# A fused attention and soft-MoE kernel: ScalarE takes a part of the reads of a shared PSUM tile, and a transpose gets 64 columns

## The chip, the cores and the metric

The kernel runs on one core of one Trainium2 chip. A core has a matrix engine (TensorE, PE in the profile, whose weight loads are listed as PEld), a vector engine (VectorE, DVE), a scalar engine (ScalarE, ACT), GpSimd (POOL), and SyncE (SP), which here only issues transfers. Each engine works through its own queue in order and waits for others on semaphores. TensorE writes its products into PSUM, from where VectorE or ScalarE carry them into SBUF.

The metric is the time of one execution on the device in microseconds (us), lower being better; the time before is the median of three runs.

## What is computed

Attention over 8 batches of 12 heads, 448 tokens and 64 columns a head, and then a soft mixture of experts over all 8 x 448 = 3,584 tokens of 768 columns. Cut to what matters:

```python
scores = q @ k.T / 8, masked above the diagonal
x = softmax(scores) @ v                      # (3584, 768), the heads side by side
logits = x @ phi                             # phi is 768 x 32
d = exp(logits - logits.max(0)); d /= d.sum(0) + 1e-09
slot_input = d.T @ x                         # 32 slots, 4 for each of 8 experts
slot_out[e] = relu(slot_input[e] @ w1[e]) @ w2[e]
c = exp(logits - logits.max(1)); c /= c.sum(1) + 1e-09
out = c @ slot_out                           # (3584, 768)
```

The first softmax of the logits runs over all tokens, so the kernel keeps a running maximum, a running sum and a running `d.T @ x` from batch to batch, and rescales them.

## The kernel before

The 96 heads are worked in 48 pairs; `block(p)` handles pair p, and six pairs make a batch. Every call on an engine goes through a helper in line 67 that keeps program order, so all rows of the profile name line 67, and one goes by the names of tiles.

A block does the following for its two heads. The scores stand in three PSUM tiles `s0`, `s1`, `s2` of 1,024 f32 columns, taken in turn. A first round of products (`scores1`, rows `s<-tri,identb` for the mask and `s<-qd,ks` for the scores) starts two heads ahead; VectorE takes column maxima out of it (`max_keys`, rows `r<-s`), TensorE turns them (`max_row`, rows `rt<-ident,r` and `s<-ident,r`), VectorE makes the row maximum (`mr`), GpSimd spreads it (`max_spread`), and a second round of products (`scores2`, rows `s<-r,k`) subtracts it within PSUM. ScalarE takes the exponential (`exps`, rows `pt<-s`), TensorE multiplies with v (`attv_pair`, rows `po<-va,pt`), VectorE divides by the sums (`norm`) and writes `x`. A block begins with the `s<-r,k` products of its first head: its head, below.

Of each finished pair, x is turned so that logits can be taken: `xtrans` makes four transposes of 128 x 128 into the PSUM tile `xm`, each with a part of x as the weights and the identity as what is moved, and `xcopy` carries 512 columns into `xt` in SBUF by ScalarE. A pair has 448 tokens: the last of the four parts of x has 64 rows and zeros below.

**The shared tile.** After the second head's exponential its score tile is free for a short while. Under the name `m = s_[(a + 1) % 3]` it takes the small products at the end of the block, and the next block then overwrites it with `scores1`, beginning with the mask `s<-tri`. What m holds goes by p % 6, from the second batch on; `mr` reads it in every block, first of all:

| p % 6 | products in m | read by VectorE after `mr` |
|---|---|---|
| 0 | sum over tokens for the previous batch's second half (`dispatch_a`, `s<-x,gs`), 384 columns from 0 | `dispatch_b`: `si`, 384 columns |
| 1, 5 | logits of two pairs (`logits_a`), columns 0 to 127 | `logits_t`: adds them to `lt` |
| 2 | turned `gs` and `lt` (`logits_e`) | copies into `gs` and `lg` |
| 3 | logits of the first two pairs; sum over tokens, first 128 columns of the first half, from column 512 | `lt` = logits + `mk` (which holds the mask of the last 64 tokens), then `si`, 128 columns |
| 4 | sum over tokens, the other 256 columns, from 512 | `si`, 256 columns |

The turned maxima for `mr` stand in the last 128 columns. `dispatch_b` computes `si = si * al + m`. The rows for p % 6 = 0 and 4 with sums occur six times each (p = 12 to 42 and 10 to 40), those of 3 seven times (p = 9 to 45). The last pair has a function of its own, `last_block`.

What orders the work is program order on each engine, and semaphores that the build puts between engines wherever two of them use one tile.

The first 24 pieces of the expert weights are loaded during the blocks. The others go into memory that the attention part frees: their transfers wait for its last products and then run one after the other to the end of the expert part. After `early.close()` a filler tile `pad` of `PAD` columns stands ahead of them.

Of the kernel before, what the change touches and what calls it, by code (L numbers as in the profile page):

```python
# [9 lines left out]
F32 = mybir.dt.float32  # L10
F32R = mybir.dt.float32r
BF16 = mybir.dt.bfloat16
AF = mybir.ActivationFunctionType
ALU = mybir.AluOpType
# [3 lines left out]
P = 128  # L18
NB, NH, S, HD = 8, 12, 448, 64
# [7 lines left out]
NCH = 4  # L27
# [6 lines left out]
NR, XB, XT = 2, 3, 2  # L34
RES, TW1, LATE2 = 24, 11, 4

HT = 2
WN, PAD = 1536, 192
WARM = (2, 3, 3)
START = (9, 6, 2, 4)  # L40

# [41 lines left out]
def attention_soft_moe(ctx: ExitStack, tc: tile.TileContext, qk, va, phi, w, out):  # L83
    nc = _Core(tc)
    const = ctx.enter_context(tc.tile_pool(name="const", bufs=1, side="left"))
# [4 lines left out]
    xtp = early.enter_context(tc.tile_pool(name="xtp", bufs=1, side="right"))  # L90
# [22 lines left out]
    x_[1] = moe.tile([P, NCH, 3 * P], F32, name="x1")  # L113
    x_[2] = moe.tile([P, NCH, 3 * P], F32, name="x2")
    x_[0] = moe.tile([P, NCH, 3 * P], F32, name="x0")
    ltn = moe.tile([P, P + 1], F32, name="lt")
    lt = ltn[:, 0:P]
    gs = moe.tile([P, P], F32, name="gs")
    mk = moe.tile([P, P], F32, name="mk")

    st = {"w": 0}
# [69 lines left out]
    ident = const.tile([P, P], F32, name="ident")  # L191
# [15 lines left out]

    for x in (x_[1], x_[0], x_[2]):
        nc.vector.memset(x[:, NCH - 1], 0.0)
    nc.scalar.activation(out=identb, in_=ident, func=AF.Copy)  # L210
    load_qk(2, 0)
    nc.gpsimd.memset(r2[0:64, :, :].bitcast(F32), 0.0)
# [210 lines left out]
    def xtrans(p):  # L423
        x, xm = st.pop(("x", p)), misc(f"xm{p}")
        st["xm", p] = xm
        for c in range(NCH):
            nc.tensor.transpose(out=xm[:, P * c:P * c + P], in_=x[:, c], identity=ident)

    def xcopy(p):
        xt = st["xt", p] = xtp.tile([P, 512], F32, tag="xt", name=f"xts{p}", bufs=XT)  # L430
        if p == NPAIR - 3:
            nc.vector.tensor_copy(out=xt, in_=st.pop(("xm", p)))
        else:
            nc.scalar.activation(out=xt, in_=st.pop(("xm", p)), func=AF.Copy)

    def logits_a(b, js, g, first=True, last=True):

# [5 lines left out]

    def logits_t(j, g):

        nc.vector.tensor_tensor(out=lt, in0=g, in1=lt if j else mk, op=ALU.add)

    def logits_b(b):

# [36 lines left out]
    def dispatch_b(b, hf, sp, sl=slice(0, 384)):  # L486
        s = si[:, 384 * hf + sl.start:384 * hf + sl.stop]
        nc.vector.scalar_tensor_tensor(out=s, in0=s, scalar=st["al", b][:, 0:1], in1=sp[:, 0:sl.stop - sl.start],
                                       op0=ALU.mult, op1=ALU.add)
# [8 lines left out]
    phis = [const.tile([P, 3, NSLOT], F32, tag="ph", name=f"phi{hf}", bufs=2) for hf in range(2)]  # L498
    run_m = [const.tile([P, 1], F32, name=f"run_m{i}") for i in range(2)]
    run_z = const.tile([P, 1], F32, name="run_z")  # L500
    lg = const.tile([P, NB, NCH, NSLOT], F32, name="lg")


# [16 lines left out]
    copy_k2(0, h0)  # L520
    sub_k(0, h0, nc.vector)
    nc.vector.memset(pob, 0.0)
    for t, v in ((mk, 0.0), (mk[96:P, 64:P], -1.0e30), (ltn[:, P:P + 1], -1.0e30), (run_m[1], 1.0e30), (run_z, 0.0)):
        nc.vector.memset(t, v)
    sub_q(0, h0)
    scores1_all(0)
# [37 lines left out]
    def block(p):  # L564
        a, b = 2 * p, p // 6 - 1
        m6 = p % 6
        if p + 1 < NPAIR:
            loads_v(p + 1, nc.sync if p + 1 < NPAIR - 1 else nc.scalar)
        if p % 2 and p < 44 or p in (16, 30):
            load_w(st["w"])  # L570
            st["w"] += 1

        if p:
            norm(p - 1, 2)
        scores2(a, range(NCH))
        exps(a)
        if p == 0:
            copy_k2(0, h1)
            cast_q(1, h1)
            warm(START[3], pob)  # L580
            max_row(1, 0)
            max_row(1, 1)
            max_spread(1)
            sub_k(1, h1, nc.vector)
        elif p > 1:
            xcopy(p - 2)
            if p == NPAIR - 2:
                sub_q(p + 1, h0)
        scores1_all(a + 2)
        if p == 0:  # L590
            warm(START[2], pob)
        for k in range(3):
            max_keys(a + 2, k)
        if p == 0:
            cast_k(2, h0)
        scores2(a + 1, range(NCH))
        exps(a + 1)
        if p == 0:
            cast_k(2, h1)
        scores1_all(a + 3)  # L600
        if m6 == 2 and p > 6:
            logits_b(b)
        max_keys(a + 3, 0)
        late_k = p == 1
        if p == 1:
            sub_q(2, h0)
            sub_k(3, h0)
            sub_q(2, h1)
            load_qk(4, 0)
        elif p:  # L610
            sub_k(p + 2, h0 if late_k else slice(0, 2))
            if not late_k:
                load_qk(p + 4, 1)
            sub_q(p + 1, h1 if p == NPAIR - 2 else slice(0, 2))
            load_qk(p + 3, 0)
        else:
            sub_q(1, h0)
            sub_q(1, h1)
            load_qk(3, 0)
            sub_k(2, h0)  # L620
        copy_k2(p + 1)
        if m6 == 2 and p > 6:
            logits_d(b, lt)
        if p:
            cast_k(p + 3)
            cast_q(p + 2)
        else:
            cast_q(2)
            cast_k(3)
        if m6 == 3 and p > 6:  # L630
            logits_al(b)
        elif m6 == 4 and p > 6:
            logits_n(b)
        attv_pair(p)
        max_row(a + 2, 1)
        max_spread(a + 2)
        if p == 0:
            sub_k(2, h1)
            load_qk(4, 1)
        for k in (1, 2):  # L640
            max_keys(a + 3, k)
        for k in range(2):
            norm(p, k)

        m = s_[(a + 1) % 3]
        parts = []
        if m6 in (1, 3, 5) and p > 1:
            j = (m6 + 3) % 6
            logits_a(b if m6 == 1 else p // 6, (j, j + 1), m[:, 0:P])
        elif m6 == 2 and p > 6:  # L650
            logits_e(b, m, 0)
        if m6 == 3 and p > 6:
            parts = [(b, 0, slice(0, P), 512)]
        elif m6 == 4 and p > 6 and p < NPAIR - 2:
            parts = [(b, 0, slice(P, 3 * P), 512)]
        elif m6 == 0 and p > 6:
            parts = [(b - 1, 1, slice(0, 3 * P), 0)]
        for d, hf, sl, o in parts:
            dispatch_a(d, hf, m[:, o:o + sl.stop - sl.start], sl)
        max_row(a + 3, 0, to=m[:, 1024 - P:1024])  # L660
        max_row(a + 3, 1)
        if m6 == 2 and p > 6:
            logits_e(b, m, 1)
        max_spread(a + 3)
        if late_k:
            sub_k(p + 2, h1)
            load_qk(p + 4, 1)
        if m6 in (1, 3, 5) and p > 1:
            logits_t(j, m[:, 0:P])
        for d, hf, sl, o in parts:  # L670
            dispatch_b(d, hf, m[:, o:o + sl.stop - sl.start], sl)
        if p:
            xtrans(p - 1)

# [7 lines left out]
    i, b, p = NHD - 1, NB - 1, NPAIR - 1  # L682
# [5 lines left out]
    x, sm = x_of(p), moe.tile([P, 2 * NCH], F32, tag="sm", name=f"sm{i}", bufs=2)  # L688
# [17 lines left out]
    for c in range(NCH):  # L706
        n = P if c < NCH - 1 else AW
        nc.scalar.activation(out=x[0:n, c, 0:HD], in_=pa[0:n, c, 0:HD], func=AF.Copy, scale=sa[0:n, c:c + 1])
    xtrans(p - 1)
    xcopy(p - 1)  # L710
    xa = xtp.tile([P, 512], F32, tag="xt", name="xta", bufs=XT)

    def last_xt(k):
        for c in (2 * k, 2 * k + 1):
# [294 lines left out]
```

## Time and profile before

| | us |
|---|---|
| median of three runs | 395.83 (395.76 to 396.35) |
| the profiled execution | 396.08 |
| its span in the profile | 394.4 |
| mean granted TensorE clock | 0.979 of full speed |

The blocks end near 300 us in the span; the expert part follows. A block takes about 6 us. In a row of the timeline the first number is the start in us from the beginning of the span, the second the length in us, then come the engine, the line, the operation, output<-input by the names of tiles, the shapes, and, in brackets, how long the engine stood idle ahead of it and which instruction seems to have ended that. In a row of the groups the count stands after x, then the busy time in us, the mean length of one in ns, and the idle time ahead. A plain f32 product is listed as two records, a transpose as one.

### The profile page before, as it was taken

Reading aid. Unit: us, or ns where it says so; the run is one execution under the profiler, and the core shown is the slowest. Engines: PE = TensorE matmul, PEld = TensorE weight load, DVE = VectorE, ACT = ScalarE, POOL = GpSimd, SP = SyncE. Lnnn points to the kernel's source line nnn. Section 1 sums busy time; section 2 is a strip of 40 time slices with the busy share of each in tenths; the row PEclk is TensorE's granted clock in tenths of the full one; section 3 lists DMA queues with packets and bytes.
Section 4 is the critical chain, followed back from the end, with each engine's and each line's share of the span. In section 5 each row is a group of like instructions: output and inputs, shape, how many; then the busy total and the mean of one; then the engine's idle time right before and its main releaser. Section 6 shows DMA issues by size and latency. Waiting matters only on the chain.

```text
span 394.4 us, 13997 instructions
## 1 busy us (share of the span) xinstructions
PE 366.3 (93%) x5763; PEld 293.9 (75%) x5763; DVE 295.2 (75%) x835; ACT 282.9 (72%) x397; POOL 256.5 (65%) x215
## 2 busy tenths in 40 slices
PE   7899999999999999999999999999999989988940
PEld 3689889888988998898889888988986544533420
DVE  7887889888888888898888988888886675342550
ACT  5888899898898898888988988888864012431440
POOL 5998899898898888898988988889860000000000
PEclk9999999999999999999999999999999999998985
DMA  7868877788898788777997877887579999999996
GB/s 250 277 229 281 288 288 237 251 273 274 274 318 272 244 270 300 257 246 248 307 323 256 286 240 249 275 287 250 183 246 399 422 431 428 429 421 419 433 429 295
DMA packets 28720, 119.17 MB, mean 302 GB/s; under 512 B 3440, under 2 KB 3952, under 8 KB 26480
## 3 DMA queue, kind: packets, MB, share of 16 engines
q1 hardware_dynamic: 28512, 118.01, 83.2%
q8 instruction: 45, 0.74, 0.7%
q10 hardware_dynamic: 144, 0.27, 0.2%
q14 instruction: 19, 0.16, 0.1%
HBM read 107.25 MB, written 11.01 MB: 300 GB/s over the span
## 4 chain that ended last, share of the span: by engine, by line
PE 67%; DMA 9%; POOL 9%; DVE 5%; ACT 4%; issue 2%; SPq 0%; POOLq 0%; DVEq 0%; ACTq 0%
PE s L67 34%; PE po L67 20%; DMA w<-in_w_dram 8%; POOL r L67 6%; PE xm L67 4%; POOL ks L67 3%; PE so L67 2%; PE e L67 2%; PE pp L67 2%; PE rt L67 2%; DMA kraw<-in_qk_dram 1%; ACT qd L67 1%; DVE lm L67 1%; DVE lg L67 1%; ACT w L67 1%
## 5 line engine op out<-in xcount | busy, mean ns | idle before, releaser
L67 DVE TRANSPOSE_TENSOR_REDUCE r<-s 128x32 f32<-128x1024 f32 x96 | 119.5, 1245 | 7.7 <-PE s L67 4.9
L67 ACT ACTIVATE pt<-s 128x1024 f32<-128x1024 f32 x96 | 98.8, 1029 | 31.0 <-PE s L67 24.0
L67 PEld LDWEIGHTS po<-va,pt 128*64 128x64 f32 x3008 | 102.3, 138 | 11.8 <-issue 11.3
L67 PE MATMUL po<-va,pt 128*64 128x65 f32 x3008 | 109.2, 224 | 0.0
L67 POOL TENSOR_TENSOR r<-qraw,qd 64x896 fp32r<-64x896 f32 (+1 forms) x50 | 99.4, 1989 | 1.9 <-ACT qd L67 1.8
L67 POOL TENSOR_TENSOR ks<-kraw,ks 64x896 fp32r<-64x896 f32 (+1 forms) x48 | 89.7, 1870 | 4.1 <-ACT ks L67 0.5
L67 POOL TENSOR_SCALAR_AFFINE_SELECT r<-mr 14x448 fp32r<-14x448 f32 x96 | 61.6, 643 | 32.9 <-DVE mr L67 28.6
L67 PE MATMUL s<-qd,ks 128*66 128x64 f32 (+3 forms) x384 | 80.6, 321 | 0.0
L67 PE MATMUL s<-r,k 128*128 128x448 f32 (+3 forms) x384 | 65.2, 291 | 2.7 <-POOL r L67 2.7
L67 PEld LDWEIGHTS s<-r,k 128*128 128x128 f32 (+1 forms) x384 | 59.3, 176 | 8.6 <-POOL r L67 5.9
L67 PEld LDWEIGHTS s<-qd,ks 128*128 128x128 f32 (+1 forms) x384 | 52.5, 183 | 2.1 <-issue 0.9
L67 ACT ACTIVATE ks<-kraw 128x896 fp32r<-128x896 f32 (+1 forms) x49 | 45.0, 920 | 5.6 <-DMA kraw<-in_qk_dram 4.4
L67 ACT ACTIVATE k<-ks 64x896 fp32r<-64x896 f32 (+1 forms) x49 | 45.8, 936 | 1.2
L67 ACT ACTIVATE qd<-qraw 128x896 fp32r<-128x896 f32 (+1 forms) x48 | 44.6, 929 | 0.9 <-POOL r L67 0.7
L67 PE MATMUL s<-tri,identb 128*128 128x192 bf16 x192 | 39.6, 270 | 0.6
L67 DVE TENSOR_REDUCE r<-r 128x16 f32<-128x32 f32 x192 | 33.7, 176 | 5.0
L67 DVE TENSOR_REDUCE mr<-s 14x32 f32<-14x128 f32 x47 | 13.1, 279 | 21.4 <-ACT qd L67 14.8
L67 PE MATMUL xm<-ident,x 128*128 128x128 f32 x188 | 28.3, 273 | 0.0
L67 ACT ACTIVATE xts<-xm 128x512 f32<-128x512 f32 x46 | 27.2, 591 | 0.4 <-PE xm L67 0.4
L67 DVE TENSOR_SCALAR x<-po,sm 64x64 f32<-64x64 f32 x94 | 25.9, 276 | 0.7
L67 DVE COPY w<-pp 128x384 f32<-128x384 f32 x28 | 14.5, 553 | 15.4 <-PE pp L67 15.3
L67 DVE TENSOR_TENSOR x<-po,sm 128x384 f32<-128x384 f32 x47 | 25.2, 537 | 0.0
(151 smaller groups left out, 397.9 us busy)
## 6 DMA issues: line engine op xcount, KB each, us to landing
w<-in_w_dram SPq DMA_DIRECT2D x34, 768.0 KB, 6.7
kraw<-in_qk_dram SPq DMA_DIRECT2D x46, 448.0 KB, 4.4
qraw<-in_qk_dram SPq DMA_DIRECT2D x46, 448.0 KB, 4.5
w<-in_w_dram SPq DMA_DIRECT2D x5, 3072.0 KB, 25.0
va<-in_va_dram SPq DMA_DIRECT2D x47, 260.0 KB, 4.8
out_dram<-w SPq DMA_DIRECT2D x7, 1536.0 KB, 12.6
w<-in_w_dram SPq DMA_DIRECT2D x5, 1536.0 KB, 11.2
qk<-in_qk_dram SPq DMA_DIRECT2D x2, 448.0 KB, 7.1
```

Source lines behind the costliest of these rows:

```text
L67: return self._tc.keep_in_program_order(op(*args, **kwargs))
```

## The change

The reads of m are split between two engines, some additions are put off, and the fourth transpose of x is made narrower.

- **Logits.** For the first two pairs of a batch (p % 6 = 3) ScalarE copies the logits from m into `lt`, in place of VectorE's addition of `mk`. The mask is put in a block later, as a memset of `lt[96:P, 64:P]` by VectorE (p % 6 = 4). The two memsets that filled `mk` at the start go.
- **Sums over tokens.** VectorE adds the first 128 columns into `si` out of m. The others (128 columns at p % 6 = 4, 256 at p % 6 = 0) ScalarE copies into a new tile `scr` in SBUF, and VectorE adds them in the next block, after `norm`'s first two steps and ahead of `mr`.
- **Transpose.** The fourth part of x is turned by a plain f32 product with 64 columns of the identity in place of a transpose with 128; `xcopy` carries 448 columns. The `xt` tiles are two fixed ones, whose last 64 columns are zeroed at the start.
- `PAD` goes from 192 to 128 columns. The transfers of the late weights wait for the same instructions in both.

```diff
-WN, PAD = 1536, 192
+WN, PAD = 1536, 128
...
+    xt_ = [xtp.tile([P, 512], F32, name=f"xt{k}") for k in range(XT)]
...
+    for x in xt_:
+        nc.vector.memset(x[:, S:], 0.0)
...
         for c in range(NCH):
-            nc.tensor.transpose(out=xm[:, P * c:P * c + P], in_=x[:, c], identity=ident)
+            if c < NCH - 1:
+                nc.tensor.transpose(out=xm[:, P * c:P * c + P], in_=x[:, c], identity=ident)
+            else:
+                nc.tensor.matmul(xm[:, P * c:S], x[:, c], ident[:, 0:S - P * c], start=True, stop=True)
...
-        xt = st["xt", p] = xtp.tile([P, 512], F32, tag="xt", name=f"xts{p}", bufs=XT)
+        xt = st["xt", p] = xt_[p % XT]
...
-            nc.scalar.activation(out=xt, in_=st.pop(("xm", p)), func=AF.Copy)
+            nc.scalar.activation(out=xt[:, 0:S], in_=st.pop(("xm", p))[:, 0:S], func=AF.Copy)
...
-        nc.vector.tensor_tensor(out=lt, in0=g, in1=lt if j else mk, op=ALU.add)
+        if j:
+            nc.vector.tensor_tensor(out=lt, in0=g, in1=lt, op=ALU.add)
+        else:
+            nc.scalar.activation(out=lt, in_=g, func=AF.Copy)
...
+    scr = const.tile([P, 2 * P], F32, name="scr")
...
-    for t, v in ((mk, 0.0), (mk[96:P, 64:P], -1.0e30), (ltn[:, P:P + 1], -1.0e30), (run_m[1], 1.0e30), (run_z, 0.0)):
+    for t, v in ((ltn[:, P:P + 1], -1.0e30), (run_m[1], 1.0e30), (run_z, 0.0)):
...
+        for d, hf, sl in st.pop("rest", ()):
+            dispatch_b(d, hf, scr, sl)
+        if m6 == 4:
+            nc.vector.memset(lt[96:P, 64:P], -1.0e30)
...
         for d, hf, sl, o in parts:
-            dispatch_b(d, hf, m[:, o:o + sl.stop - sl.start], sl)
+            n = sl.stop - sl.start - P
+            dispatch_b(d, hf, m[:, o:o + P], slice(sl.start, sl.start + P))
+            if n:
+                nc.scalar.activation(out=scr[:, 0:n], in_=m[:, o + P:o + P + n], func=AF.Copy)
+                st["rest"] = ((d, hf, slice(sl.start + P, sl.stop)),)
```

How the instructions stand after the build is shown at two places. A bracket names the semaphores that an instruction waits for, each by the engine or the transfer queue that raises it (`DVE_49` is raised by VectorE, `Activation_49` by ScalarE).

The first place is the seam from pair 30 (p % 6 = 0) to pair 31; m is `s_80` there. On ScalarE before, from the end of pair 30's casts into pair 31:

```order
L67 ACTIVATE k_92<-ks_87 64x2x448
L67 ACTIVATE ks_87<-kraw_83 128x2x448 [waits DMAHW4_49,PE_49,Activation_49]
L67 ACTIVATE qd<-qraw_84 128x896 [waits DMAHW5_49,Pool_49]
L67 ACTIVATE pt_94<-s_81 128x1024 [waits DVE_49,PE_49]
L67 ACTIVATE xts_3271<-xm_3256 128x512
```

and with the change:

```order
L67 ACTIVATE qd<-qraw_84 128x896 [waits DMAHW5_49,Pool_49]
L67 ACTIVATE scr<-s_80 128x256 [waits DVE_49,PE_49]
L67 ACTIVATE pt_94<-s_81 128x1024 [waits PE_49]
L67 ACTIVATE xt_101<-xm_3250 128x448
L67 ACTIVATE pt_95<-s_79 128x1024 [waits PE_49]
```

The copy into `scr` stands between the cast of `qd` and the new block's exponential, and waits for VectorE; the value that it waits for is that of VectorE's 128-column sum out of the same tile. On TensorE before, at the same seam, from the head to the overwriting of m:

```order
L67 MATMUL s_81<-r_93,k_92 128x448 [waits Activation_49,Pool_49]
L67 MATMUL s_81<-r_93,k_92 128x320
L67 MATMUL s_81<-r_93,k_92 128x192
L67 MATMUL s_81<-r_93,k_92 66x64
L67 LDWEIGHTS identb
L67 MATMUL s_80<-tri_117,identb 128x192 [waits DVE_49]
```

and with the change, from the last use of m in pair 30 on:

```order
L67 MATMUL s_80<-ident,r_91 76x128 [waits DVE_49]
L67 MATMUL xm_3250<-ident,x_99 128x128 [waits PE_49]
L67 MATMUL xm_3250<-ident,x_99 128x128 x2
L67 MATMUL xm_3250<-ident,x_99 128x64
L67 MATMUL s_81<-r_93,k_92 128x448 [waits Activation_49,Pool_49]
L67 MATMUL s_81<-r_93,k_92 128x320
L67 MATMUL s_81<-r_93,k_92 128x192
L67 MATMUL s_81<-r_93,k_92 66x64
L67 LDWEIGHTS identb
L67 MATMUL s_80<-tri_119,identb 128x192 [waits Activation_49]
```

The mask product that overwrites m now waits for ScalarE's copy, where it waited for VectorE's sum; and the fourth product of `xm` has 64 columns.

The second place is the end of pair 33 (p % 6 = 3); m is again `s_80`. On VectorE before:

```order
L67 RECIPROCAL sm_3539<-sm_3539 128x7 [waits DVE_49]
L67 TENSOR_REDUCE mr_3555<-s_80 14x32 [waits PE_49,Activation_49,Pool_49]
L67 TENSOR_TENSOR lt<-s_80,mk 128x128
L67 SCALAR_TENSOR_TENSOR si<-si,al_3498,s_80 128x128 [waits Activation_49]
L67 TENSOR_TENSOR x_98<-po,sm_3539 128x2x3x64 [waits DVE_49]
```

and with the change, VectorE first:

```order
L67 RECIPROCAL sm_3531<-sm_3531 128x7 [waits DVE_49]
L67 TENSOR_REDUCE mr_3547<-s_80 14x32 [waits PE_49,Activation_49,Pool_49]
L67 SCALAR_TENSOR_TENSOR si<-si,al_3490,s_80 128x128 [waits Activation_49]
L67 TENSOR_TENSOR x_98<-po,sm_3531 128x2x3x64 [waits DVE_49]
L67 TENSOR_SCALAR x_98<-po,sm_3531 64x64 x2
```

then ScalarE at the same place:

```order
L67 ACTIVATE qd<-qraw_88 128x896 [waits DMAHW0_49,Pool_49]
L67 ACTIVATE al_3490<-run_m_150,run_m_149 128x1
L67 ACTIVATE lt<-s_80 128x128 [waits DVE_49]
L67 ACTIVATE pt_94<-s_81 128x1024 [waits PE_49]
L67 ACTIVATE xt_100<-xm_3552 128x448
```

The addition into `lt` has left VectorE's queue, and ScalarE's copy waits for VectorE's `mr`. VectorE's sum waited for ScalarE before too, for `al`; with the change the value that it waits for is that of the copy into `lt`.

More of the change, by code (lines that the diff above doesn't have):

```diff
@@ L426, in xtrans @@
         for c in range(NCH):
-            nc.tensor.transpose(out=xm[:, P * c:P * c + P], in_=x[:, c], identity=ident)
+            if c < NCH - 1:
+                nc.tensor.transpose(out=xm[:, P * c:P * c + P], in_=x[:, c], identity=ident)
+            else:
+                nc.tensor.matmul(xm[:, P * c:S], x[:, c], ident[:, 0:S - P * c], start=True, stop=True)
     def xcopy(p):
-        xt = st["xt", p] = xtp.tile([P, 512], F32, tag="xt", name=f"xts{p}", bufs=XT)
+        xt = st["xt", p] = xt_[p % XT]
         if p == NPAIR - 3:
-            nc.vector.tensor_copy(out=xt, in_=st.pop(("xm", p)))
+            nc.vector.tensor_copy(out=xt[:, 0:S], in_=st.pop(("xm", p))[:, 0:S])
         else:
-            nc.scalar.activation(out=xt, in_=st.pop(("xm", p)), func=AF.Copy)
+            nc.scalar.activation(out=xt[:, 0:S], in_=st.pop(("xm", p))[:, 0:S], func=AF.Copy)
     def logits_a(b, js, g, first=True, last=True):
@@ L710, in attention_soft_moe @@
     xcopy(p - 1)
-    xa = xtp.tile([P, 512], F32, tag="xt", name="xta", bufs=XT)
+    xa = xt_[p % XT]
     def last_xt(k):
```

## The prediction

> **What bounds the kernel now.** First the head of the page.
>
> ```profile
> span 394.4 us, 13997 instructions
> PE 366.3 (93%) x5763; PEld 293.9 (75%) x5763; DVE 295.2 (75%) x835; ACT 282.9 (72%) x397; POOL 256.5 (65%) x215
> PE 67%; DMA 9%; POOL 9%; DVE 5%; ACT 4%; issue 2%; SPq 0%; POOLq 0%; DVEq 0%; ACTq 0%
> ```
>
> The span and the shares of the chain that ended last say: TensorE is the bound, with other engines in the chain for short pieces. The profiled execution took 396.08 us, 1.7 more than its span; the median is 395.83. After the last block the chain is one long stretch of weights.
>
> ```profile
> 326.46 30.39 DMA w<-in_w_dram
> ```
>
> Those loads start as attention lets go of its buffers, so whatever the blocks lose or win moves the end by as much. The question is what one block loses. The next view is the timeline around the seam from pair 30 (p%6 = 0) to pair 31, columns start, length, engine.
>
> ```profile
> 197.49 0.30 PE L67 MATMUL s<-ident,r 128*76 128x128 f32 x1
> 197.52 0.47 PEld L67 LDWEIGHTS xm<-ident,x 128*128 128x128 f32 x4
> 197.93 0.28 DVE L67 TENSOR_REDUCE mr<-s 14x32 f32<-14x128 f32 x1 [0.72 <-ACT qd L67]
> 197.99 0.71 PE L67 MATMUL s<-r,k 128*128 128x448 f32 x4
> 198.14 0.59 DVE L67 SCALAR_TENSOR_TENSOR si<-si,al,s 128x384 f32<-128x384 f32 x1
> 198.78 0.24 PE L67 MATMUL s<-tri,identb 128*128 128x192 bf16 x1
> ```
>
> The first row is the old block's last use of the shared tile m; 0.50 later the new block's head (`s<-r,k`) starts, and then the mask product `s<-tri` must overwrite m. It starts at 198.78, 0.05 after VectorE's sum ends at 198.73: VectorE's reading of m holds TensorE. An unheld seam, pair 31 to 32:
>
> ```profile
> 203.62 0.31 PE L67 MATMUL s<-ident,r 128*76 128x128 f32 x1
> 204.12 0.72 PE L67 MATMUL s<-r,k 128*128 128x448 f32 x4
> 204.28 0.27 DVE L67 TENSOR_TENSOR lt<-s,lt 128x128 f32<-128x128 f32 x1
> 204.68 0.26 PE L67 MATMUL s<-tri,identb 128*128 128x192 bf16 x1
> ```
>
> Here m is free at 204.55, and the mask comes at 204.68, 0.56 after the head and 1.06 after `s<-ident,r`: TensorE's own pace. Counted from `s<-ident,r`, the mask of pair 31 comes at 1.29, so it loses 0.23. The other two seams with sums, 33 to 34 and 34 to 35:
>
> ```profile
> 215.56 0.30 PE L67 MATMUL s<-ident,r 128*76 128x128 f32 x1
> 216.00 0.28 DVE L67 TENSOR_REDUCE mr<-s 14x32 f32<-14x128 f32 x1 [0.73 <-ACT qd L67]
> 216.21 0.27 DVE L67 TENSOR_TENSOR lt<-s,mk 128x128 f32<-128x128 f32 x1
> 216.41 0.33 DVE L67 SCALAR_TENSOR_TENSOR si<-si,al,s 128x128 f32<-128x128 f32 x1
> 216.79 0.24 PE L67 MATMUL s<-tri,identb 128*128 128x192 bf16 x1
> ```
>
> ```profile
> 221.62 0.30 PE L67 MATMUL s<-ident,r 128*76 128x128 f32 x1
> 222.06 0.37 ACT L67 ACTIVATE run_z<-run_z,bs,al 128x1 f32<-128x1 f32 x1
> 222.07 0.28 DVE L67 TENSOR_REDUCE mr<-s 14x32 f32<-14x128 f32 x1 [0.51 <-ACT qd L67]
> 222.28 0.46 DVE L67 SCALAR_TENSOR_TENSOR si<-si,al,s 128x256 f32<-128x256 f32 x1
> 222.79 0.24 PE L67 MATMUL s<-tri,identb 128*128 128x192 bf16 x1
> ```
>
> Masks 1.23 and 1.17 after `s<-ident,r`: losses of 0.17 and 0.11. These three waits, six or seven times each, are all that the split of the reads can win: 6 x 0.23 + 7 x 0.17 + 6 x 0.11 = 3.2 us.
>
> **The reads, part by part.** The rows of the built order decide. ScalarE's copy `scr<-s` waits for VectorE and PE, `lt<-s` waits for VectorE, and the mask of pair 31 now waits for ScalarE. The two engines do not read m side by side: each waits for the other's read. The shortened VectorE sum is followed by a ScalarE copy in line. Prices:
>
> ```profile
> L67 ACT ACTIVATE xta<-e 128x256 f32<-128x256 f32 x1 | 0.4, 377 | 0.0
> L67 ACT ACTIVATE mk<-e 128x128 f32<-128x128 f32 x1 | 0.3, 277 | 0.2 <-PE e L67 0.2
> 310.95 0.29 DVE L67 TENSOR_TENSOR lg<-lg,lm 128x128 f32<-128x128 f32 x1
> 311.28 0.31 ACT L67 ACTIVATE lg<-lg 128x128 f32<-128x128 f32 x1 [1.71 <-DVE lg L67]
> 311.62 0.29 DVE L67 TENSOR_REDUCE lm<-lg 128x4 f32<-128x128 f32 x1 [0.37 <-ACT lg L67]
> ```
>
> A sum of 128 columns takes 0.33 (the row at 216.41), ScalarE's PSUM copies 0.38 (256 columns) and 0.28 (128). The other rows price a hand-over: 311.28 − 311.24 = 0.04 to ScalarE, 311.62 − 311.59 = 0.03 back; to TensorE 0.05, as above.
>
> - 30 to 31: sum 198.14 to 198.47; ScalarE 198.51 to 198.89; mask 198.94 instead of 198.78: **+0.16**, 6 times.
> - 33 to 34: `mr` ends 216.28; `lt` copy 216.32 to 216.60; VectorE's sum, which waits for ScalarE, 216.63 to 216.96; mask 217.01 instead of 216.79: **+0.22**, 7 times.
> - 34 to 35: sum 222.28 to 222.61; ScalarE (its queue is free at 222.43) 222.65 to 222.93; mask 222.98 instead of 222.79: **+0.19**, 6 times.
>
> Together 0.96 + 1.54 + 1.14 = 3.6 us. Queued behind each copy on ScalarE is the new block's exponential, which needs the head's products (0.71 from the head, the row at 197.99); the copies end 0.90, 0.54 and 0.81 after a head that stands 0.50 behind `s<-ident,r`. So it starts at most 0.2 late, still no later than the mask, and I take the mask's delay alone. Were a hand-over free, each seam would lose 0.04 to 0.07 less; twice as long, as much more.
>
> The sums put off (`si<-si,al,scr`) stand ahead of `mr`, in the 0.51 to 0.73 that VectorE idles there: 0.46 for 256 columns by the row of 34 to 35 fits, and so do 128 columns and the mask's memset. Without that cover `mr` would come later by what sticks out, under 0.1 six times.
>
> **The fourth transpose.** It becomes a plain f32 product. In the trace transposes are one record each (188 for 47 calls), but a plain f32 product is two records with two weight loads:
>
> ```profile
> 308.70 0.30 PEld L67 LDWEIGHTS e<-rz,srep 128*128 128x128 f32 x2 [0.41 <-issue]
> L67 PEld LDWEIGHTS e<-rz,srep 128*128 128x128 f32 x2 | 0.3, 188 | 0.4 <-issue 0.4
> L67 PE MATMUL e<-rz,srep 128*128 128x1 f32 x2 | 0.4, 260 | 0.0
> L67 PE MATMUL xm<-ident,x 128*128 128x128 f32 x188 | 28.3, 273 | 0.0
> ```
>
> The four `xm` loads above last 0.47 with 0.14 each: one per 0.11. The two loads of one plain product, 128 weights wide and with a single column moved, take 0.30 with 0.19 each, again one per 0.11. So with weights this wide the load sets the pace, however few columns move; two loads replace one: **+0.11**. The other end is 0: two passes of 64 columns cost what one of 128 did, if columns set the pace. I take 0.11, since the `e<-rz` row moves fewer columns still and is no faster.
>
> [...]
>
> Where this 0.11 lands: at the three held seams it hides, because `mr` and the sums start from `s<-ident,r`, ahead of the transposes, and 198.94 − 197.49 = 1.45 (1.45 and 1.36 for the others) exceeds 1.06 + 0.11. It counts at p%6 = 5 to 0, 6 times: 0.66. From p%6 = 1 to 3 it passes through ScalarE:
>
> ```profile
> 209.55 0.94 ACT L67 ACTIVATE qd<-qraw 128x896 fp32r<-128x896 f32 x1
> 210.54 0.25 PE L67 MATMUL s<-qd,ks 128*66 128x64 f32 x1
> L67 ACT ACTIVATE xts<-xm 128x512 f32<-128x512 f32 x46 | 27.2, 591 | 0.4 <-PE xm L67 0.4
> L67 ACT ACTIVATE ct<-cp 128x448 fp32r<-128x448 f32 x6 | 3.0, 559 | 0.0
> ```
>
> Pair 33's first score waits for `qd` (210.49 plus 0.05), whose chain begins at pair 32's head: +0.11, less 0.03 for copying 448 columns instead of 512, 7 times: 0.56. In the first batch it hides behind GpSimd:
>
> ```profile
> 52.32 0.60 PE L67 MATMUL xm<-ident,x 128*128 128x128 f32 x4
> 53.09 0.47 PE L67 MATMUL s<-r,k 128*128 128x448 f32 x1 [0.17 <-POOL r L67]
> ```
>
> The head comes 0.77 after the transposes' start, against 0.36 at pair 31, so 0.41 is spare. Two last transposes, 0.22.
>
> At the start two small memsets join VectorE's queue and two of `mk` leave it; the chain there runs through the input, so I take 0, with 0.2 the other end.
>
> **Sum:** 3.6 + 0.66 + 0.56 + 0.22 = 5.1 us on 396.08; on the median, **400.9 us**.
>
> **Rivals.**
> - *Columns set the pace of the fourth transpose.* Then its 0.11 is 0 and the 0.03 of the shorter copy stays: 3.6 − 0.2 = 3.4, 399.2 us. For it: the output is half as wide. Against: `e<-rz`. Chance 0.19.
> - *The copy of `lt` is not held.* The tile has two halves of 512 columns, `lt` in the first, `mr` and that sum in the second. If ScalarE ran beside VectorE there, 33 to 34 would have the sum at 216.21 to 216.54 and the mask at 215.56 + 1.17 = 216.73: −0.06 instead of +0.22, so 5.1 − 7 x 0.28 = 3.1, 398.9 us. Against: `lt<-s` waits for VectorE in the order. Chance 0.05. [...]
> - *Faster: VectorE's shorter read frees m, and ScalarE's copy ends before the head's products do.* Then the mask is at TensorE's pace at all three seams, 3.2 won, plus 0.2, if the transpose costs nothing: 392.4 us. It decides the sign when copies end less than 0.56 after the head; by the rows they end 0.90, 0.54 and 0.81 after it, and the middle one has a sum to follow. Chance 0.07.
> - *The change does little:* waits and gains cancel, 395.8 us, chance 0.04.
> - *More than forecast,* hand-overs twice as long and late exponentials: some 0.1 more at each of 19 seams, 1.9 in all, 402.8 us. Chance 0.05.
>
> **The numbers.** The forecast has 0.60. The range takes in the first two rivals and, above, part of the last: 398.6 to 402.3. Less than 0.2%, 0.8 us, cannot be told from no change. Faster 0.07, same 0.04, slower 0.89.
>
> **What would show it.** In the timeline, the mask after seams 0 to 1, 3 to 4 and 4 to 5 released by ScalarE or by a sum that follows it, 1.45, 1.45 and 1.36 after `s<-ident,r`; ScalarE idle ahead of `scr` and `lt`, released by VectorE; `xm` with five loads in some 0.6. `xm` loads of four, or a mask 1.06 after `s<-ident,r` at these seams, would prove it wrong.

## The result, and the profile after

The changed kernel takes **402.15 us** (median of 4 runs, 401.83 to 402.24), the kernel before beside it 396.01 (395.76 to 396.35): ratio 1.0151, 95% interval 1.0138 to 1.0164. It is 6.1 us slower. The profiled execution took 401.83 us. From its page, the head and the shares of the chain that ended last:

```profile
span 400.1 us, 14110 instructions
PE 370.2 (93%) x5810; PEld 298.8 (75%) x5810; DVE 296.1 (74%) x847; ACT 287.1 (72%) x417; POOL 256.9 (64%) x215
...
PE 66%; ACT 9%; DMA 8%; DVE 6%; issue 3%; POOL 3%; DVEq 0%; ACTq 0%; POOLq 0%
```

TensorE's share is the same 93%, but in the chain ScalarE went from 4% to 9%, and GpSimd from 9% to 3%. What ScalarE and VectorE wait for at the new instructions is in the view of waits (total us, times, longest):

```profile
ACT scr L67 <- DVE si L67: 6.9, 12, 1.0
DVE si L67 <- ACT lt L67: 2.4, 7, 0.3
ACT lt L67 <- DVE mr L67: 2.3, 8, 0.3
PE s L67 <- ACT scr L67: 1.3, 6, 0.4
```

Twelve copies `scr`, all of them released by VectorE's `si`; seven sums released by ScalarE's `lt`; TensorE released by `scr`. The timeline of the changed kernel shows how these stand one behind the other; rows in between that the argument does not need are left out. A seam is the passage from one block to the next, named by p % 6; at a held seam (0 to 1, 3 to 4, 4 to 5) the mask waits for a read of m. Seam 0 to 1 (pair 36 to 37):

```profile
237.82 0.30 PE L67 MATMUL s<-ident,r 128*76 128x128 f32 x1
237.86 0.63 PEld L67 LDWEIGHTS xm<-ident,x 128*128 128x128 f32 x5
238.27 0.28 DVE L67 TENSOR_REDUCE mr<-s 14x32 f32<-14x128 f32 x1 [0.72 <-PE s L67]
238.44 0.71 PE L67 MATMUL s<-r,k 128*128 128x448 f32 x4
238.47 0.33 DVE L67 SCALAR_TENSOR_TENSOR si<-si,al,s 128x128 f32<-128x128 f32 x1
238.90 0.38 ACT L67 ACTIVATE scr<-s 128x256 f32<-128x256 f32 x1 [0.77 <-DVE si L67]
239.18 1.03 ACT L67 ACTIVATE pt<-s 128x1024 f32<-128x1024 f32 x1
239.33 0.24 PE L67 MATMUL s<-tri,identb 128*128 128x192 bf16 x1 [0.19 <-ACT scr L67]
```

`xm` has five weight loads in 0.63 where there were four in 0.47, so the head `s<-r,k` comes 0.62 behind `s<-ident,r`, where it was 0.50. VectorE's sum ends at 238.80, ScalarE starts at 238.90, and the mask product comes at 239.33, 1.51 after `s<-ident,r`, where it was 1.29. Seam 3 to 4 (33 to 34), then 4 to 5 (34 to 35):

```profile
219.02 0.30 PE L67 MATMUL s<-ident,r 128*76 128x128 f32 x1
219.46 0.28 DVE L67 TENSOR_REDUCE mr<-s 14x32 f32<-14x128 f32 x1 [0.73 <-PE s L67]
219.77 0.28 ACT L67 ACTIVATE lt<-s 128x128 f32<-128x128 f32 x1 [0.29 <-DVE mr L67]
220.08 0.35 DVE L67 SCALAR_TENSOR_TENSOR si<-si,al,s 128x128 f32<-128x128 f32 x1 [0.34 <-ACT lt L67]
220.49 0.24 PE L67 MATMUL s<-tri,identb 128*128 128x192 bf16 x1
```

```profile
225.31 0.30 PE L67 MATMUL s<-ident,r 128*76 128x128 f32 x1
225.76 0.28 DVE L67 TENSOR_REDUCE mr<-s 14x32 f32<-14x128 f32 x1 [0.33 <-ACT qd L67]
225.97 0.33 DVE L67 SCALAR_TENSOR_TENSOR si<-si,al,s 128x128 f32<-128x128 f32 x1
226.38 0.28 ACT L67 ACTIVATE scr<-s 128x128 f32<-128x128 f32 x1 [0.33 <-DVE si L67]
226.71 0.24 PE L67 MATMUL s<-tri,identb 128*128 128x192 bf16 x1
```

Masks 1.47 and 1.40 after `s<-ident,r`; before 1.23 and 1.17. The last `mr` is put down to `qd`, and with that the chain, followed back from there, runs through ScalarE's exponentials, its copy of `xm` and its casts, 4.1 us of ScalarE between 219 and 226. Two of its pieces (start, length):

```profile
224.75 0.94 ACT qd L67
...
225.76 0.28 DVE mr L67
```

That is a releaser by coincidence: `qd` ends 0.07 ahead of `mr`, but `mr` starts 0.41 to 0.45 after `s<-ident,r` in every pair from 6 on, of before and of after, whenever `qd` ends. So most of the growth to 9% is not the price of the copies. At 33 to 34 VectorE, free at 219.74, waits until ScalarE's copy of `lt` ends at 220.05, and starts at 220.08. At none of the three seams shown do the two engines read m at the same time.

All runs are compared by one table: the start of the mask minus the start of `s<-ident,r` at each kind of seam (median over all seams from pair 6 on, from the timelines, us), and the time from the head of pair 0 to the head of pair 47. That second number comes from one profiled execution each; it leaves out the start of the program, which differed by up to 0.7 us between them, and the weights after the last block. The kernel before was run again beside each group of experiments, at 395.67 to 395.95, so medians of different groups compare to some 0.3 us.

| kernel | 0→1 | 1→2 | 2→3 | 3→4 | 4→5 | 5→0 | head 0 to head 47 | median us |
|---|---|---|---|---|---|---|---|---|
| before | 1.30 | 1.05 | 1.22 | 1.23 | 1.17 | 1.04 | 284.50 | 396.01 |
| after | 1.51 | 1.17 | 1.14 | 1.47 | 1.40 | 1.17 | 290.39 | 402.15 |
| e1, four full transposes | 1.51 | 1.05 | 1.22 | 1.47 | 1.40 | 1.05 | 289.35 | 400.79 |
| e2, `lt` on VectorE | 1.51 | 1.17 | 1.14 | 1.23 | 1.40 | 1.17 | 289.44 | 401.13 |
| e9, e2 with four memsets more | 1.50 | 1.17 | 1.14 | 1.23 | 1.40 | 1.17 | 288.61 | 400.66 |
| e3, sums on VectorE | 1.30 | 1.17 | 1.14 | 1.47 | 1.17 | 1.17 | 287.36 | 398.74 |
| e5, ScalarE alone reads | 1.30 | 1.06 | 1.22 | 1.47 | 1.19 | 1.05 | 286.66 | 397.68 |
| e4, transpose part alone | 1.30 | 1.17 | 1.14 | 1.23 | 1.17 | 1.16 | 286.21 | 397.03 |
| e11, plain, 128 columns | 1.30 | 1.17 | 1.14 | 1.23 | 1.17 | 1.16 | 285.74 | 396.82 |
| e12, plain, 16 columns | 1.30 | 1.16 | 1.14 | 1.23 | 1.17 | 1.16 | 285.68 | 397.88 |
| e7, copy of 448 alone | 1.30 | 1.05 | 1.22 | 1.23 | 1.16 | 1.05 | 284.51 | 395.74 |
| e8, transpose of 64 rows | 1.35 | 1.33 | 1.30 | 1.35 | 1.35 | 1.33 | 291.99 | 403.05 |

Before and after differ by 5.89 between the two heads. By seams, after minus before: 0→1 6 x 0.21, and 0.20 once more at pair 30 (1.46); 3→4 7 x 0.24 (1.68); 4→5 6 x 0.23 (1.38); 5→0 6 x 0.13 (0.78); 1→2 and 2→3 together 7 x 0.04 (0.28). `s<-ident,r` itself comes 0.03 later after the mask in the blocks of p%6 = 1 and 5, 12 x 0.03 (0.36). That is 5.94. After the last head the two executions differ by 0.18 (100.43 and 100.25), too little against the 99.1 to 101.3 of all twelve to be read.

### The profile page after: what moved, and what is told of

It is laid out like the page before. It is cut to its first block, busy times and chain, and to the rows that moved or that the text cites. A ratio compares the mean times of both kernels' runs of the same rounds, so it can differ in the third digit from the quotient of the medians.

```text
span 400.1 us, 14110 instructions
## 1 busy us (share of the span) xinstructions
PE 370.2 (93%) x5810; PEld 298.8 (75%) x5810; DVE 296.1 (74%) x847; ACT 287.1 (72%) x417; POOL 256.9 (64%) x215
## 4 chain that ended last, share of the span: by engine, by line
PE 66%; ACT 9%; DMA 8%; DVE 6%; issue 3%; POOL 3%; DVEq 0%; ACTq 0%; POOLq 0%
PE s L67 32%; PE po L67 20%; DMA w<-in_w_dram 8%; PE xm L67 4%; ACT pt L67 3%; PE e L67 2%; PE so L67 2%; PE pp L67 2%; POOL r L67 2%; ACT qd L67 2%; PE rt L67 2%; ACT k L67 1%; DVE lm L67 1%; POOL ks L67 1%; PE warm L67 1%
## 5 line engine op out<-in xcount | busy, mean ns | idle before, releaser
L67 PEld LDWEIGHTS po<-va,pt 128*64 128x64 f32 x3008 | 102.3, 138 | 11.8 <-issue 11.5
L67 PE MATMUL xm<-ident,x 128*128 128x128 f32 (+1 forms) x235 | 31.1, 263 | 0.0
L67 PEld LDWEIGHTS xm<-ident,x 128*128 128x128 f32 x235 | 29.6, 161 | 0.1
```

What stands on the lines that cost most here:

```text
L67: return self._tc.keep_in_program_order(op(*args, **kwargs))
```

## The experiments

Three theories are put against each other.

- Theory A: the reads of m stand in line, ScalarE behind VectorE and TensorE behind both, and the fourth product's second weight load is a smaller term by itself.
- Theory B: the fourth product makes most of the loss.
- Theory C: the added work on ScalarE delays its exponentials, and so TensorE.

`PAD` stays at 128 in all runs but e5. e7, which has that `PAD` and the new tiles and otherwise only the shorter copy, takes as long as the kernel before, so `PAD` has no part in the loss.

**e1: the changed kernel with four full transposes.**

```diff
-            if c < NCH - 1:
-                nc.tensor.transpose(out=xm[:, P * c:P * c + P], in_=x[:, c], identity=ident)
-            else:
-                nc.tensor.matmul(xm[:, P * c:S], x[:, c], ident[:, 0:S - P * c], start=True, stop=True)
+            nc.tensor.transpose(out=xm[:, P * c:P * c + P], in_=x[:, c], identity=ident)
```

> The changed kernel with all four transposes of x as before (128 columns each, true transposes); ScalarE's copies of lt and scr, the late sums and the 448-column copy of xm stay. Theory A (reads of m stand in line: ScalarE behind VectorE, the mask product behind ScalarE; the fourth product's second weight load is a separate, smaller term): from `s<-ident,r` to the next head back from 0.61 to 0.50; seams 5 to 0 and 1 to 2 back to a mask 1.05 after `s<-ident,r`; the three held seams keep 1.51, 1.47 and 1.40 within 0.03. Gain 6 x 0.12 + 7 x 0.07 + 0.22 = 1.4 us: 400.7 us (400.4 to 401.0). Theory B (the fourth transpose makes most of the loss): 397 us or less. Theory C (more work on ScalarE delays the exponentials and so TensorE, not the release of m): 400.7 too, but with waits of TensorE for `pt` that the kernel before does not have.

400.79 us (400.20 to 400.84), ratio 1.0123 (1.0106 to 1.0140). 1.36 won of the median, 1.04 between the heads; the unheld seams are back at 1.05, and the held ones keep 1.51, 1.47 and 1.40 to the hundredth. B falls: most of the loss is still there. C asked for waits of TensorE for `pt`; the view of waits lists none, here as in the kernels before and after.

**e2: the changed kernel with `lt` on VectorE.**

```diff
-        if j:
-            nc.vector.tensor_tensor(out=lt, in0=g, in1=lt, op=ALU.add)
-        else:
-            nc.scalar.activation(out=lt, in_=g, func=AF.Copy)
+        nc.vector.tensor_tensor(out=lt, in0=g, in1=lt if j else mk, op=ALU.add)
```

> The changed kernel with the copy of lt back as VectorE's addition of mk, as before, and without the late memset of lt; all else as changed. Theory A: the seam 3 to 4 alone changes, its mask back from 1.47 to 1.23 after `s<-ident,r`; the seams 0 to 1 and 4 to 5 keep 1.51 and 1.40. Gain 7 x 0.24 = 1.7 us: 400.5 us (400.2 to 400.8). Theory B: no change beyond 0.3 us, 402 us. Theory C: the gain is not at that seam, or is spread over the others.

401.13 us (400.97 to 401.22), ratio 1.0134 (1.0118 to 1.0150): 1.0 won, not the 1.7 expected, and outside the 400.2 to 400.8 given. Yet the seam did what A said: 3→4 went back to 1.23 and the others did not move. The gain at 7 seams is there, and 0.7 is lost elsewhere: against the changed kernel the masks come 0.15 later at pair 30, 0.15 at 37, 0.20 at 38 (behind 37) and 0.16 at 44. VectorE in the timeline of e2, the end of pair 30 and of pair 37:

```profile
199.79 0.20 DVE L67 RECIPROCAL sm<-sm 128x7 f32<-128x7 f32 x1
201.06 0.28 DVE L67 TENSOR_REDUCE mr<-s 14x32 f32<-14x128 f32 x1 [1.07 <-PE xm L67]
...
243.78 0.43 DVE L67 SCALAR_TENSOR_TENSOR si<-si,al,scr 128x256 f32<-128x256 f32 x1
244.72 0.28 DVE L67 TENSOR_REDUCE mr<-s 14x32 f32<-14x128 f32 x1 [0.51 <-ACT qd L67]
```

`s<-ident,r` started at 200.26 and 243.93, so `mr` comes 0.80 and 0.79 after it, where all other pairs have 0.41 to 0.45. Counted from 0 over all of VectorE's records in the trace, its waits included, these two are number 575 and 703, 128 apart. (At pair 44 it is number 831, the copy into `gs`, that starts 0.18 late.) In the changed kernel number 575 is the `si` of pair 30, 0.11 after the end of `mr` where pair 36's starts 0.08 ahead of that end, and its mask comes 1.71 after `s<-ident,r`, not 1.51: the 0.20 extra in the sum above.

**e9: e2 with four small memsets on VectorE in block 2,** to move what stands at those numbers.

```diff
+        if p == 2:
+            for _ in range(4):
+                nc.vector.memset(ltn[:, P:P + 1], -1.0e30)
```

> As e2 (lt on VectorE), with four small memsets of VectorE more in block 2, where VectorE waits for TensorE. e2 gained 1.0 us and not 1.7: in its trace `mr` comes 0.80 and 0.79 after `s<-ident,r` in pairs 30 and 37 (0.45 elsewhere), and these two are number 575 and 703 of VectorE's records, 128 apart; other kernels show single gaps at the same numbers. Theory S (VectorE stops for 0.2 to 0.45 at fixed numbers of its instruction stream, and what it costs depends on what stands there): with four instructions more the stops fall ahead of the wait for `s<-ident,r`; `mr` comes at 0.45 in pairs 30 and 37, and 0.5 to 0.7 us is won: 400.5 us (400.3 to 400.8). Rival (the late `mr` belongs to those pairs, by their DMAs or another engine): no change, 401.1 us, `mr` late in the same two pairs.

400.66 us (399.27 to 400.98), ratio 1.0110 (1.0091 to 1.0128). VectorE in e9 at the same two places:

```profile
199.82 0.20 DVE L67 RECIPROCAL sm<-sm 128x7 f32<-128x7 f32 x1
200.74 0.28 DVE L67 TENSOR_REDUCE mr<-s 14x32 f32<-14x128 f32 x1 [0.72 <-PE s L67]
...
243.45 0.43 DVE L67 SCALAR_TENSOR_TENSOR si<-si,al,scr 128x256 f32<-128x256 f32 x1
244.04 0.28 DVE L67 TENSOR_REDUCE mr<-s 14x32 f32<-14x128 f32 x1 [0.16 <-ACT qd L67]
```

`mr` is back at 0.44 in both pairs. The median's 0.5 lies within its runs' spread of 1.7, but between the heads e9 is 0.83 shorter than e2, and 1.78 shorter than the changed kernel. Of this 0.20 is the late `si` of pair 30, which went too; what is left agrees, to 0.1, with the 7 x 0.24 that A gives the copy of `lt`. Four instructions more made this one execution shorter between the heads.

**e3: the changed kernel with the dispatch sums in one piece on VectorE.**

```diff
-            n = sl.stop - sl.start - P
-            dispatch_b(d, hf, m[:, o:o + P], slice(sl.start, sl.start + P))
-            if n:
-                nc.scalar.activation(out=scr[:, 0:n], in_=m[:, o + P:o + P + n], func=AF.Copy)
-                st["rest"] = ((d, hf, slice(sl.start + P, sl.stop)),)
+            dispatch_b(d, hf, m[:, o:o + sl.stop - sl.start], sl)
```

> The changed kernel with the dispatch sums back in one piece on VectorE straight from PSUM (384 and 256 columns, no scr, no late sums); the copy of lt on ScalarE and the narrow fourth product stay. Theory A: the masks of the seams 0 to 1 and 4 to 5 back to 1.30 and 1.17 to 1.20 after `s<-ident,r`; 3 to 4 keeps 1.47. Also back: the 0.03 between mask and next `s<-ident,r` in the two blocks that hold the late sums. Gain 6 x 0.21 + 6 x 0.21 + 12 x 0.03 = 2.9 us: 399.3 us (398.9 to 399.8). Theory B: no change beyond 0.3 us. Theory C: up to 2.9 us too, but the masks at the two seams move by less than 0.1.

398.74 us (397.99 to 399.80), ratio 1.0076 (1.0052 to 1.0100), just below the 398.9 to 399.8 given: 3.4 won of the median, 3.03 between the heads, where 2.9 was expected; the 0.20 at pair 30 went too. The masks are back at 1.30 and 1.17 and 3→4 keeps 1.47. C wanted them to move by less than 0.1; they moved by 0.21 and 0.23. Between the heads the three parts undone singly, 1.04 (e1), 1.78 (e9) and 3.03 (e3), make 5.85 of 5.89; the 0.20 of pair 30 is in both e9 and e3, and counted once they make 5.65. The 6 x 0.03 in the blocks of p%6 = 5, which none of the three brings back, is most of what is missing.

**e5: ScalarE reads all of the dispatches, VectorE nothing of them.** Is it a copy on ScalarE that costs, or two reads one behind the other? The kernel is that of e1, with `PAD` 56 and a wider `scr` in the place of `mk`; what changes in the reads:

```diff
-            parts = [(b, 0, slice(P, 3 * P), 512)]
+            parts = [(b, 0, slice(P, 3 * P), 0)]
...
-            dispatch_b(d, hf, m[:, o:o + P], slice(sl.start, sl.start + P))
-            if n:
-                nc.scalar.activation(out=scr[:, 0:n], in_=m[:, o + P:o + P + n], func=AF.Copy)
-                st["rest"] = ((d, hf, slice(sl.start + P, sl.stop)),)
+            if n == P:
+                dispatch_b(d, hf, m[:, o:o + P], sl)
+            else:
+                nc.scalar.activation(out=scr[:, 0:n], in_=m[:, o:o + n], func=AF.Copy)
+                st["rest"] = ((d, hf, sl),)
```

(n is the whole piece here.)

> As e1 (four full transposes, copy of lt on ScalarE), but at the seams 0 to 1 and 4 to 5 ScalarE copies all 384 or 256 columns of the dispatches into scr and VectorE reads nothing of them in m; its sum of the whole piece comes later, from scr. Theory A (the two reads stand in line, so one read of more columns ends earlier than a read of 128 followed by a copy of the rest): mr ends 0.73 after `s<-ident,r`, the hand-over is 0.08 to 0.10, the copy 0.49 (384 columns, between 0.38 for 256 and 0.54 for 448) or 0.38, TensorE follows 0.05 later: masks at 1.35 and 1.24 in place of 1.51 and 1.40; 3 to 4 keeps 1.47. Against e1 6 x 0.16 + 6 x 0.16 = 1.9 us won: 398.9 us (398.3 to 399.4). Rival (a copy on ScalarE is what costs, whoever else reads): masks no earlier than 1.45 and 1.36, 400.5 us.

397.68 us (397.58 to 398.13), ratio 1.0046 (1.0032 to 1.0060): faster than expected by 1.2, and below the 398.3 to 399.4 given. Its timeline at pair 36 to 37:

```profile
235.71 0.30 PE L67 MATMUL s<-ident,r 128*76 128x128 f32 x1
236.15 0.28 DVE L67 TENSOR_REDUCE mr<-s 14x32 f32<-14x128 f32 x1 [0.72 <-ACT qd L67]
236.47 0.49 ACT L67 ACTIVATE scr<-s 128x384 f32<-128x384 f32 x1 [0.40 <-DVE mr L67]
237.01 0.24 PE L67 MATMUL s<-tri,identb 128*128 128x192 bf16 x1
```

One copy of 384 columns frees m 1.25 after `s<-ident,r`, and the mask comes at 1.30, as with VectorE's one sum before the change. So ScalarE reading is not the price; two reads of the sums, one behind the other, are. The masks came 0.05 earlier than expected by the hand-over: 0.04 from `mr` to `scr` here (236.43 to 236.47), where `si` to `scr` took 0.10 (238.80 to 238.90) and I had expected the same. These 12 x 0.05 and the 0.20 of pair 30 are what e5 is ahead of the expected between the heads; the rest of the 1.2 is not between the heads of this execution. As a version it has no gain: the seams stand where they stood, and `lt` still costs its 1.7.

**e4: the transpose part alone on the kernel before.** Its edit is the change's hunks on `xt_`, `xtrans` and `xcopy`; `PAD` is 128, and `scr` is there unused.

> The kernel before with the transpose part of the change alone: the fourth product of 64 columns and the copy of 448 columns into fixed tiles; lt, the dispatch sums and mk on VectorE as before. Theory A: the held seams hide the 0.11, their masks stay at 1.30, 1.23 and 1.17; seams 5 to 0 and 1 to 2 go to 1.17. Loss over before 6 x 0.12 + 7 x 0.04 + 0.22 = 1.2 us: 397.2 us (396.8 to 397.6). Theory B: most of the 6.1 us, 400 us or more. If the 64 columns saved as much as the second load costs (columns set the pace): no loss, 396.0 us or less.

397.03 us (396.63 to 397.53; 8 runs), ratio 1.0032 (1.0021 to 1.0043): 1.2 over before, as expected. The held seams keep 1.30, 1.23 and 1.17 and hide the 0.11. Between the heads it is 1.71, of which 0.5 lies in the first block of this execution alone (7.98 us; 7.46 before); the same in e11 and e12 is 1.24 and 1.18.

**e11 and e12: is it the loads or the columns?** Both are e4 with another fourth product: a plain f32 product of all 128 columns, and of 16. e12 leaves the last 48 tokens of each pair out of x transposed, and ScalarE copies 400 columns there.

```diff
-                nc.tensor.matmul(xm[:, P * c:S], x[:, c], ident[:, 0:S - P * c], start=True, stop=True)
+                nc.tensor.matmul(xm[:, P * c:P * c + P], x[:, c], ident, start=True, stop=True)
```

```diff
-                nc.tensor.matmul(xm[:, P * c:S], x[:, c], ident[:, 0:S - P * c], start=True, stop=True)
+                nc.tensor.matmul(xm[:, P * c:S - 48], x[:, c], ident[:, 0:16], start=True, stop=True)
```

> The kernel before with the copy of 448 columns, and the fourth product as a plain f32 product of all 128 columns (two weight loads), not narrowed. Theory A (the weight loads set the pace, 0.11 each, however few columns move): from `s<-ident,r` to the next head 0.61, as with 64 columns; 397.0 us (396.6 to 397.5), as the run with the transpose part alone. Rival (columns set the pace, and the narrowing to 64 had paid for a part of the second pass): twice 128 columns in place of twice 64, 0.05 per pass by the two passes of 64 whose matmuls stand 0.058 apart in the changed kernel: 0.70 or more, 398.2 us.

> As the run with the transpose part alone, but the fourth product moves 16 columns in place of 64 (and ScalarE copies 400 columns in place of 448): the last 48 tokens of each pair are left out of x transposed, their columns stay 0. Theory A (the weight loads set the pace): from `s<-ident,r` to the next head 0.61 still; 397.0 us (396.6 to 397.5). Rival (columns set the pace): 0.04 less for each of the two passes, 0.53, about 396.0 us.

Groups of instructions by shape (busy, mean ns of one), of e11 and then of e12, behind them two rows of e12's timeline:

```profile
L67 PEld LDWEIGHTS xm<-ident,x 128*128 128x128 f32 x235 | 29.6, 161 | 0.1
L67 PE MATMUL xm<-ident,x 128*128 128x128 f32 x235 | 33.6, 274 | 0.0
```

```profile
L67 PEld LDWEIGHTS xm<-ident,x 128*128 128x128 f32 x235 | 29.6, 161 | 0.1
L67 PE MATMUL xm<-ident,x 128*128 128x16 f32 x94 | 13.8, 222 | 0.0
228.37 0.30 PE L67 MATMUL s<-ident,r 128*76 128x128 f32 x1
228.98 0.71 PE L67 MATMUL s<-r,k 128*128 128x448 f32 x4
```

235 loads in 47 calls, five each, in both; the records of the products get shorter, from 274 to 222 ns, and nothing follows from that: with 128, 64 and 16 columns the head comes 0.61 after `s<-ident,r`. So the columns do not set the pace. A pass is one load and one product, and these two runs alone would also allow a fixed price of a pass; against that, the 3,008 loads of 64 weight columns for `po<-va,pt` in the kernel before take 102.3 us, 0.034 a pass. So the loads of 128 are what is left to set the pace here: those of `xm` start 0.11 us apart, in the kernel before as in the changed one (0.109 and 0.110 on the median), while the records themselves are longer (141 and 161 ns on the mean). e11 takes 396.82 us (396.38 to 397.71), ratio 1.0033 (1.0019 to 1.0047), as expected. e12 takes 397.88 (396.87 to 398.30), ratio 1.0052 (1.0031 to 1.0072), 0.9 more than expected and above the range given; its heads are as far apart as e11's, so the excess lies outside the blocks (its profiled execution has 101.3 us behind the last head, e11's 99.6), and its cause stays open.

**e7: the copy of 448 columns alone, with four full transposes.** Its edit is the change's hunks on `xt_` and `xcopy`, with `PAD` and `scr` as in e4.

> The kernel before with one thing of the change: the copy of xm takes 448 columns into two fixed tiles whose last 64 columns are cleared once. Four full transposes, all reads of m on VectorE. Theory A (ScalarE's copy is on the chain from pair p%6 = 1 to 3): the seam 2 to 3 goes from 0.64 to 0.58 or less between `s<-ident,r` and head, 7 x 0.05 = 0.3 us won, 395.5 us (395.2 to 395.9). If the 0.03 more between mask and `s<-ident,r` in blocks of p%6 = 5, which all kernels with this copy show, comes from it: 0.2 given back. Rival (the copy is hidden): 395.8 us.

395.74 us (394.93 to 396.27; 11 runs), ratio 0.9993 (0.9984 to 1.0002), and 284.51 between the heads against 284.50. The copy takes 537 ns instead of 591, and nothing is won: the rival was right. 2→3 did not move either, and the reason stands in the timeline of the kernel before, around the head of pair 33:

```profile
209.20 0.64 POOL L67 TENSOR_SCALAR_AFFINE_SELECT r<-mr 14x448 fp32r<-14x448 f32 x1
...
209.89 0.60 PEld L67 LDWEIGHTS s<-r,k 128*128 128x128 f32 x4 [0.17 <-POOL r L67]
```

That head waits for GpSimd, not for ScalarE.

**e8: the fourth product as a transpose of the 64 rows that hold data,** one load of 64 rows, 64 columns, and else as e7.

```diff
-            nc.tensor.transpose(out=xm[:, P * c:P * c + P], in_=x[:, c], identity=ident)
+            n = min(P, S - P * c)
+            nc.tensor.transpose(out=xm[:, P * c:P * c + n], in_=x[0:n, c], identity=ident[0:n, 0:n])
```

> As the run with the 448-column copy, and the fourth product as a true transpose of the 64 rows that hold data (64 rows by 128 weights, 64 columns moved, one weight load). Theory A (a load of 128 weights sets the pace of these products, 0.11 each, however few columns move): from `s<-ident,r` to head 0.50 as with four full transposes, 395.5 us (395.2 to 395.9). Rival (columns set the pace, and the second load alone was what cost): 0.45 or less, so another 13 x 0.05 = 0.6 us won, 394.9 us.

403.05 us (402.58 to 404.03), ratio 1.0183 (1.0169 to 1.0197). Neither of the two came: this one edit costs more than the whole change. TensorE and its loads in e8 at pair 36 to 37:

```profile
239.45 0.30 PE L67 MATMUL s<-ident,r 128*76 128x128 f32 x1
239.49 0.36 PEld L67 LDWEIGHTS xm<-ident,x 128*128 128x128 f32 x3
...
240.01 0.14 PEld L67 LDWEIGHTS xm<-ident,x 64*128 64x128 f32 x1 [0.17 <-issue]
240.21 0.60 PEld L67 LDWEIGHTS s<-r,k 128*128 128x128 f32 x4
```

The three full loads end at 239.85; the load of 64 rows starts 0.16 later, and the next full load 0.20 after that one's start, where the others stand 0.11 apart. The head comes 0.76 after `s<-ident,r`, 0.26 later than with four full transposes, at nearly every seam, and the masks 0.05 to 0.28 later. Why the load of 64 rows starts late no run here shows. So e8 could not tell columns from loads, which e11 and e12 then did.

No run here is faster than the kernel before by more than its interval. Whether the two engines could read m side by side if the build did not put them in line was not tried.

## Why the prediction was right

The forecast was 400.9 us in a range of 398.6 to 402.3; the median is 402.15, inside by 0.15 only. The sum was 5.1 us, and 6.1 came. The mechanism was right and the sizes were mostly too small: 3.6 for the reads measured 4.5 between the heads, 0.66 for 5→0 measured 0.78, nothing for the way from the mask to the next `s<-ident,r` measured 0.36. One term was too large, 0.56 against 0.28, and that it made up for a part of the others is luck. The 0.22 for the last transposes cannot be read out of these runs. Point by point:

- **The reads stand in line: right, shown.** The three masks came 1.51, 1.47 and 1.40 after `s<-ident,r`, predicted 1.45, 1.45 and 1.36, all by the releasers named. The term of 3.6 measured 4.5. What was short is the hand-over: 0.04 was taken for all of them from a pair in the tail, and `si` to `scr` takes 0.08 to 0.10 (226.30 to 226.38; 238.80 to 238.90), while `mr` to `lt` takes 0.03. Another 0.20 is the late `si` at pair 30, once, which no row of before could show.
- **The fourth transpose costs its second load: right, shown** by e4, e11 and e12. From pair 7 on it is +0.11 at every head but that of 2→3, hidden at the held seams, counted at 5→0 (0.12 to 0.13 a seam). By the rival of the columns 16 would have been cheaper than 64 and 64 than 128; they are equal.
- **From p%6 = 1 to 3: the size was off and its reason wrong.** 7 x 0.08 was predicted, 7 x 0.04 came. The credit of 0.03 for the shorter copy does not exist (e7). The second block does not add the full 0.11: 2→3 falls from 1.22 to 1.14, as the head there had waited for GpSimd, and a later `s<-ident,r` uses up that wait: at pair 32 GpSimd's `r<-mr` ended 0.59 after `s<-ident,r` before, and 0.48 after it in the changed kernel.
- **The late sums cost nothing: nearly.** `mr` keeps its 0.44, but `s<-ident,r` comes 0.03 later in two blocks of six, 0.36 in all, which the sum did not have. In the blocks of p%6 = 1 it goes with the late sums: e1 and e5 have it there, e3 and e4 do not. In those of p%6 = 5 e3 and e4, which have no late sums, show it too, and e7, which has neither these nor the plain product, does not; why stays open.
- **Exponentials late by the copies: late by 0.1, at no cost that the runs show.** At seam 36 to 37 ScalarE's `pt` starts at 239.18, 1.36 after `s<-ident,r` and 0.15 ahead of the mask; before the change it was 1.25 (235.00 and 233.75). At 3→4 and 4→5 the later head makes this delay: in e1, with the head back and the copies still there, `pt` starts at 1.25. At 0→1 it stays at 1.35 in e1, so there the copy of 256 columns holds it as well. Where e3 and e9 brought a mask back, the time came back in full, so the mask's delay alone could be taken.
- **The other rivals fall.** `lt` was held by `mr`, and held `si`; no held seam came to TensorE's own pace; little change is far outside the interval. Of *more than forecast* the first half came true: a part of the hand-overs is twice as long; late exponentials add nothing.

## What to carry to other kernels

Before a read of a shared buffer is split between two engines, look in the built order whether the second reader waits for the first: if it does, the split turns one read into two plus a hand-over, 0.03 to 0.10 us here, and e5 shows that giving all of it to ScalarE ends about as early as giving all of it to VectorE (masks 1.30 and 1.19 against 1.30 and 1.17). A product narrowed to fewer columns gained nothing here, where its weight loads set the pace: with 128, 64 and 16 columns the head came 0.61 us after `s<-ident,r`, and the second load cost 0.11. In such a place, count loads, not columns. Undo the parts one at a time and compare the same seam: the parts make 5.65 of 5.89 us between the heads, while in e2 stray late starts took 0.7 off the gain in the median.

## What the runs showed of the hardware that was not expected

- VectorE starts late at a few places that go by the number of the instruction. In e2 its records 575 and 703 start 0.35 later after `s<-ident,r` than in the other pairs; four instructions more ahead of them (e9) bring both back to 0.44, as other instructions stand at these numbers then. In the changed kernel the same number 575 makes one `si` 0.19 late. Compared with the same instruction of the other batches, from the second batch on and over all twelve kernels, late starts of 0.18 us or more stand at the numbers 319 (e5), 447 (e3), 575 and 703 (the changed kernel, e1, e2) and 831 (e2) alone, each 128 from the next; the other seven kernels have none, so such a number need not bring one. The cause no run shows; what is shown is the place, and that the cost depends on what stands there.
- One load of 64 rows among loads of 128 brings the next head 0.26 us later (e8). Full loads start 0.11 apart there, under product records of 0.27; the load of 64 rows starts 0.16 after the last of them has ended, and the next full load 0.20 after its start. The cause no run shows.
